# The first out-block's weight conversion moves into the middle of attention; the second in-block's rounding goes one step later

## The chip, the core and the metric

The kernel runs on one core of a Trainium2 chip. The metric is the device time in microseconds (us). The engines are TensorE (PE; PEld is its weight load), VectorE (DVE), ScalarE (ACT), GpSimd (POOL) and SyncE (SP), whose queue issues the loads. Each has its own instruction stream and runs it strictly in order; they wait for one another by semaphores.

## What is computed

Three stages in one program, from `reference.py`, cut:

```python
# attention: q, k, v of (2, 8, 768, 64) float32, 4 sinks, window 128
scores = scale * np.matmul(q, k.transpose(0, 1, 3, 2))
keep = is_sink | in_window            # 0 <= query - key < 128, or key < 4
scores = np.where(keep, scores, -1e9)
a = softmax(scores)                   # max subtracted, 1e-9 added to the sum
x = np.matmul(a, v)                   # then to 1536 tokens x 512
# MoE layer 1: w_in 512 x 2048, w_out 2048 x 512, float64
h = np.maximum(x @ w_in, 0.0); x = h * h @ w_out
# MoE layer 2: the same shapes
h = x @ w_in; g = h * np.tanh(np.log1p(np.exp(h))); out = g @ w_out
```

## The kernel before

**Weights.** Both layers' weights are float64 in memory. The kernel takes them in blocks of 128 hidden units: per block 512 KB for the in-product (`wi`) and 512 KB for the out-product (`wo`), loaded as raw 32-bit pairs and converted on the chip into a high and a low part, so that a product is three terms (low x high, high x low, high x high) of four 128x128x512 matmuls each. Class `Conv` (L104 to L174) holds the steps of one block, each an instruction of 128x512:

- `load`: SP's DMA into tile `raw` (L113 for `wi`, L118 for `wo`; three buffers).
- `head`: ACT scales the upper words into `cv_a` (L128); `head_pool` is the same on POOL (L130).
- `mid_r1` (L136), `mid_r2` (L142), `mid_or` (L148): three on DVE, called r1, r2 and or below; they make `cv_r` (r1 the sign, r2 the top bits of the lower words) and merge it into `cv_a`. `mid_r` is r1 and r2.
- `high`: ACT rounds `cv_a` (L167; `wih` or `woh`). `low`: DVE subtracts it from `cv_a` (L171; `wil` or `wol`), after `high`.

Block 0 is the first `wi`, block 1 the first `wo`, block 2 the second `wi` (tiles `wih1`, `wil1`). All further blocks are converted by the MoE's own loop (`moe()`, L615); the framework's scheduler lets the first two of them (tiles numbered 2051 and 2053 and the `cv` tiles beside them) start on DVE and ACT between the last steps of attention.

**Attention.** 12 query tiles of 128 rows (6 of each batch), 4 pairs of heads in each, so 48 pairs; the loop at L549 runs n from -3 to 52 over them as a hand-written pipeline. In step n:

- PE computes the scores `s` of pair n + 4 (L373), ACT the exponentials `pr` of pair n + 3 (L396), with their sums, DVE the masked max of pair n + 4 (L384, two).
- At even n DVE makes `rs`, the reciprocals of the sums (L407, L408), with which POOL multiplies `pr` (L416, two). PE transposes a tile of q or of k (L323, tile `tr`), which DVE copies to `qt` (L329) or ACT to `kt` (L332); PE computes the outputs `av` of two pairs (L465).
- At odd n PE transposes `pr` of two pairs into `pt` (L428, two banks), of which ACT or DVE makes the copies `pts` (L443).
- Once per query tile ACT copies `av` to `xf` (L480), which the next tile's first `av` waits for, since `av` has one buffer. POOL splits `xf` into `xh` and `xl` (L481, L483); for the last two tiles DVE makes `xl` (L490). In the step after, SP issues the loads `qn`, `kn` and `vn` of a later tile (L232).
- `pt` and `tr` share three PSUM buffers, so a late copy of one holds up the next.

At n = 46 and 48 PE also computes the first two in-products `h` of the first 512 tokens (L195), with the weights of block 0 and of block 2; ACT takes relu, square and `gh` one step later (L204 to L206), DVE `gl` two steps later (L209). The MoE then begins with the first out-product `o` (L634), which uses block 1, and goes on with `h` and `o` in turn to the end.

**What sets the order.** The order in attention is as written in the loop; the conversion steps are called last in step n, by the table `PLAN` {block: {n: steps}} (L497). SP, ACT, DVE and POOL each get them in that order among their own work.

Of the kernel before, what the change touches and what calls it, by code (L numbers as in the profile page):

```python
# [28 lines left out]
def kernel(  # L29
# [463 lines left out]
    for fb in range(W1N):  # L493
# [2 lines left out]
    WARM = (6, 3, 2, 1)  # L496
    PLAN = {  # L497
        0: {5: "load", 11: "head", 13: "mid_r1", 15: "mid_r2", 17: "mid_or", 19: "high low"},
        2: {36: "load", 41: "head_pool", 44: "mid_r", 45: "mid_or", 46: "high low"},
        1: {37: "load", 46: "head mid_r", 47: "mid_or", 48: "high low"},  # L500
    }

    IN_AT = (46, 48)
# [519 lines left out]
```

## Time and profile before

| | |
|---|---|
| median of 3 runs | 620.19 us (619.1 to 620.61) |
| profiled execution | 619.7 us, its span 617.9 us |
| PE busy | 609.0 us (99% of the span) |
| DVE busy | 454.5 us (74%) |
| ACT busy | 351.0 us (57%) |
| POOL busy | 70.1 us (11%) |

The profiled execution's time is the span and 1.8 us around it. Busy is the time in which an engine had an instruction in work; waits of other engines cost nothing where PE does not wait for them. Attention takes about the first 95 us of the span, the two MoE layers the rest; POOL's 70.1 us lie almost all in attention.

### The profile page before, as it was taken

What the parts mean: (1) busy time and instruction counts of PE and PEld (TensorE: products, weight loads), DVE (VectorE), ACT (ScalarE), POOL (GpSimd) and SP (SyncE); (2) the same over time, 40 slices, a digit from 0 to 9 for tenths busy, and PEclk for the clock granted to TensorE, in tenths of its full rate; (3) what the DMA queues carried; (4) which work ended last, traced back from release to release, by engine and by line L of the source; (5) the groups of instructions that cost most, each with busy time, mean ns of one, the idle gap of its engine ahead of it and who ended that gap; (6) DMA issues with size and microseconds to landing.
All of it is one profiled execution on the core that took longest, in us unless ns stands there. A gap on an engine that the chain in (4) does not pass through costs nothing.

```text
span 617.9 us, 10113 instructions
## 1 busy us (share of the span) xinstructions
PE 609.0 (99%) x3774; PEld 494.5 (80%) x3774; DVE 454.5 (74%) x951; ACT 351.0 (57%) x723; POOL 70.1 (11%) x101
## 2 busy tenths in 40 slices
PE   9999999999999999999999999999999999999996
PEld 6676677888888888888888888888888888888885
DVE  5897889998921111169898789999887788887784
ACT  4888876777743233367777655555444444454442
POOL 5788870000000000000000000000000000000000
PEclk9999999999999999999999999999999999999999
DMA  9998835666600000026666400000010000010001
GB/s 190 198 191 173 185 102 185 207 201 201 198 7 1 0 2 1 1 90 186 190 186 199 137 0 2 1 0 1 1 69 0 1 0 1 28 42 1 1 0 72
DMA packets 74904, 50.24 MB, mean 81 GB/s; under 512 B 52708, under 2 KB 69348, under 8 KB 74852
## 3 DMA queue, kind: packets, MB, share of 16 engines
q1 hardware_dynamic: 74560, 49.16, 29.0%
q8 instruction: 31, 0.51, 0.4%
q10 hardware_dynamic: 292, 0.39, 0.2%
q14 instruction: 21, 0.17, 0.1%
HBM read 46.40 MB, written 3.15 MB: 80 GB/s over the span
## 4 chain that ended last, share of the span: by engine, by line
PE 96%; DVE 2%; ACT 1%; issue 0%; DVEq 0%; ACTq 0%
PE o L634 42%; PE h L195 41%; PE s L373 4%; PE av L465 3%; PE tr L323 2%; PE pt L428 2%; PE idle L529 1%; DVE cv_a L148 0%; DVE cv_r L142 0%; ACT pr L396 0%; DVE cv_r L136 0%; DVE pts L443 0%; DVE qt L329 0%; DVE s L384 0%; DVE rs L408 0%
## 5 line engine op out<-in xcount | busy, mean ns | idle before, releaser
L195 PE MATMUL h<-xh,wil 128*128 128x512 f32 x384 | 102.9, 390 | 0.0
L195 PE MATMUL h<-xl,wih 128*128 128x512 f32 x384 | 102.6, 389 | 0.0
L195 PE MATMUL h<-xh,wih 128*128 128x512 f32 x384 | 102.6, 389 | 0.0
L209 DVE TENSOR_TENSOR gl<-h,gh 128x512 fp32r<-128x512 f32 x48 | 33.2, 691 | 89.3 <-ACT gh L206 89.3
L195 PEld LDWEIGHTS h<-xl,wih 128*128 128x128 f32 x384 | 72.1, 188 | 15.0
L195 PEld LDWEIGHTS h<-xh,wih 128*128 128x128 f32 x384 | 72.1, 188 | 15.0
L195 PEld LDWEIGHTS h<-xh,wil 128*128 128x128 f32 x384 | 71.9, 188 | 14.9
L634 PE MATMUL o<-gh,wol 128*128 128x512 f32 x192 | 74.8, 389 | 0.8 <-DVE wol L171 0.8
L702 ACT ACTIVATE e<-t,small 128x512 f32<-128x512 f32 x48 | 34.8, 725 | 70.7 <-DVE t L698 70.7
L634 PE MATMUL o<-gl,woh 128*128 128x512 f32 x192 | 74.7, 389 | 0.0
L634 PE MATMUL o<-gh,woh 128*128 128x512 f32 x192 | 74.7, 389 | 0.0
L204 ACT ACTIVATE h<-h 128x512 f32<-128x512 f32 x48 | 27.9, 582 | 77.5 <-PE h L195 77.5
L634 PE MATMUL o<-wol,gh 128*128 128x512 f32 x176 | 68.5, 389 | 0.0
L634 PE MATMUL o<-woh,gl 128*128 128x512 f32 x176 | 68.5, 389 | 0.0
L634 PE MATMUL o<-woh,gh 128*128 128x512 f32 x176 | 68.5, 389 | 0.0
L718 ACT CAST gh<-t 128x512 fp32r<-128x512 f32 x44 | 27.4, 623 | 46.1 <-PE o L634 42.7
L148 DVE SCALAR_TENSOR_TENSOR cv_a<-cv_a,cv_r 128x512 int32<-128x512 int32 x64 | 45.2, 706 | 6.2
L209 DVE TENSOR_TENSOR gl<-t,gh 128x512 fp32r<-128x512 f32 x44 | 30.4, 690 | 19.5 <-ACT gh L718 19.5
L396 ACT ACTIVATE pr<-s,nm 128x208 f32<-128x208 f32 (+2 forms) x96 | 40.5, 436 | 6.1 <-DVE nm L384 5.7
L416 POOL TENSOR_TENSOR pr<-pr,rs 128x416 f32<-128x416 f32 (+2 forms) x48 | 41.5, 885 | 15.0 <-DVE rs L408 10.4
L128 ACT ACTIVATE cv_a<-raw 128x512 f32<-128x512 f32 x63 | 42.4, 675 | 0.4 <-DMA raw<-in_moe_w_in_dram 0.2
L634 PEld LDWEIGHTS o<-gh,wol 128*128 128x128 f32 x192 | 36.0, 188 | 8.2 <-PE av L465 0.9
(100 smaller groups left out, 1004.1 us busy)
## 6 DMA issues: line engine op xcount, KB each, us to landing
raw<-in_moe_w_in_dram SPq DMA_DIRECT2D x32, 512.0 KB, 4.0
raw<-in_moe_w_out_dram SPq DMA_DIRECT2D x32, 512.0 KB, 4.3
vn<-in_v_dram SPq DMA_DIRECT2D x12, 256.0 KB, 5.1
qn<-in_q_dram SPq DMA_DIRECT2D x10, 256.0 KB, 4.4
kn<-in_k_dram SPq DMA_DIRECT2D x9, 256.0 KB, 4.8
vx<-in_v_dram SPq DMA_DIRECT2D x16, 128.0 KB, 4.3
out_dram<-ob SPq DMA_DIRECT2D x8, 256.0 KB, 2.4
kn<-in_k_dram SPq DMA_DIRECT2D x6, 128.0 KB, 3.0
```

Of the source, the lines that this page charges most:

```text
L128: nc.scalar.activation(out=self.a, in_=high_words, func=AF.Copy, scale=2.0**-112)
L148: nc.vector.scalar_tensor_tensor(out=ai, in0=ai, scalar=3, in1=self.r, op0=ALU.logical_shift_left, op1=ALU.bitwise_or)
L195: nc.tensor.matmul(ph, lhsT=w[a][:, d, :], rhs=x[:, d, :], start=(m == 0 and d == 0), stop=(m == 2 and d == NDC - 1),)
L204: nc.scalar.activation(out=ph, in_=ph, func=AF.Relu)
L209: nc.vector.tensor_tensor(out=gl, in0=x, in1=f32(gh), op=ALU.subtract)
L373: nc.tensor.matmul(banks[e][qs, 0:w], lhsT=qt[b, i][r, j, qs], rhs=kt[r, j, k0 : k0 + w], start=True, stop=True, skip_group_check=True,)
L396: nc.scalar.activation(out=pr[b, i][:, 2 * j + e, 0:w], in_=banks[e][:, 0:w], func=AF.Exp, bias=nm[:, e : e + 1], scale=-1.0, accum_out=sm ...
L416: nc.gpsimd.tensor_tensor(out=x, in0=x, in1=rs.to_broadcast([P, 2, w]), op=ALU.mult)
L465: nc.tensor.matmul(av[b, i][e * D : (e + 1) * D, j, qs], lhsT=x[0:kv, 2 * j + e, :], rhs=pts[0:kv, c, e, qs], start=(j == 0 and m == 0), s ...
L634: nc.tensor.matmul(acc[sp][t], lhsT=a, rhs=x, start=(fb == 0 and m == 0), stop=(fb == NFB - 1 and m == 2),)
L702: nc.scalar.activation(out=e, in_=t, func=AF.Ln, bias=two)
L718: nc.scalar.copy(g_tiles(n)[0], et[n][1])
```

## The change

Two lines of the table. Block 1's load, head, r1, r2, or, and high and low go from steps 37 and 46 to 48 to the odd steps 25 to 33, its load to step 20; block 2's high and low go from step 46 to step 47, where they stand behind `xf` on ACT.

```diff
     PLAN = {
         0: {5: "load", 11: "head", 13: "mid_r1", 15: "mid_r2", 17: "mid_or", 19: "high low"},
-        2: {36: "load", 41: "head_pool", 44: "mid_r", 45: "mid_or", 46: "high low"},
-        1: {37: "load", 46: "head mid_r", 47: "mid_or", 48: "high low"},
+        1: {20: "load", 25: "head", 27: "mid_r1", 29: "mid_r2", 31: "mid_or", 33: "high low"},
+        2: {36: "load", 41: "head_pool", 44: "mid_r", 45: "mid_or", 47: "high low"},
     }
```

PE's and POOL's order stay as they were. In mid-attention, block 1's five instructions come into the streams of ACT and DVE. On DVE (`+` is the changed kernel's), n = 33: the low part comes between the two pairs of max.

```order
@@ -233,4 +236,5 @@
 L384 ISA s,nm<-s,mask_w 128x208
 L384 ISA nm 128x1
+L171 TENSOR_TENSOR wol_111<-cv_a,woh_110 128x512
 L384 ISA s,nm<-s,mask_w 128x208
 L384 ISA nm 128x1
```

In the same way r1, r2 and or stand between two pairs of max at n = 27, 29 and 31, and on ACT the head (n = 25) and the high part (n = 33) stand between a copy `pts` and the exponentials.

The end of attention on DVE, before, from block 2's r1 (`cv_r_1785`) on; 1936 and 1935 are block 1's tiles, 2058 is the first MoE block's, `xl2_72` the split of the last but one query tile:

```order
L136 TENSOR_SCALAR cv_r_1785<-raw_1607 128x512
L142 TENSOR_SCALAR cv_r_1785<-raw_1607 128x512
L148 SCALAR_TENSOR_TENSOR cv_a_1784<-cv_a_1784,cv_r_1785 128x512
L443 COPY pts_1900<-pt_1883 128x8x64
L171 TENSOR_TENSOR wil1_113<-cv_a_1784,wih1_112 128x512
L136 TENSOR_SCALAR cv_r_1936<-raw_1641 128x512
L136 TENSOR_SCALAR cv_r_2058<-raw_2051 128x512
L142 TENSOR_SCALAR cv_r_1936<-raw_1641 128x512
L142 TENSOR_SCALAR cv_r_2058<-raw_2051 128x512
L148 SCALAR_TENSOR_TENSOR cv_a_1935<-cv_a_1935,cv_r_1936 128x512
L490 TENSOR_TENSOR xl2_72<-xf_1940,xh2_69 128x4x128
```

The same place on DVE in the changed kernel (block 2's tiles are 1792 and 1793 here, the MoE blocks' 2057 and 2058, 2063 and 2064):

```order
L136 TENSOR_SCALAR cv_r_1793<-raw_1617 128x512
L142 TENSOR_SCALAR cv_r_1793<-raw_1617 128x512
L148 SCALAR_TENSOR_TENSOR cv_a_1792<-cv_a_1792,cv_r_1793 128x512
L136 TENSOR_SCALAR cv_r_2058<-raw_2051 128x512
L142 TENSOR_SCALAR cv_r_2058<-raw_2051 128x512
L148 SCALAR_TENSOR_TENSOR cv_a_2057<-cv_a_2057,cv_r_2058 128x512
L443 COPY pts_1908<-pt_1891 128x8x64
L136 TENSOR_SCALAR cv_r_2064<-raw_2053 128x512
L142 TENSOR_SCALAR cv_r_2064<-raw_2053 128x512
L148 SCALAR_TENSOR_TENSOR cv_a_2063<-cv_a_2063,cv_r_2064 128x512
L171 TENSOR_TENSOR wil1_113<-cv_a_1792,wih1_112 128x512
L490 TENSOR_TENSOR xl2_72<-xf_1941,xh2_69 128x4x128
```

Block 1's instructions are gone from there; the two MoE blocks' sets of r1, r2 and or now stand ahead of `wil1`, one of them ahead of the copy `pts` too.

The same place on ACT, before, from the copy `pts` ahead of block 2's high part to the relu of the first `h`:

```order
L443 COPY pts_1900<-pt_1882 128x8x64
L167 CAST wih1_112<-cv_a_1784 128x512
L128 ACTIVATE cv_a_1935<-raw_1641 128x512
L128 ACTIVATE cv_a_2057<-raw_2051 128x512
L480 COPY xf_1940<-av_1861 128x512
L128 ACTIVATE cv_a_2063<-raw_2053 128x512
L204 ACTIVATE h_1920<-h_1920 128x512
```

And in the changed kernel:

```order
L128 ACTIVATE cv_a_2057<-raw_2051 128x512
L443 COPY pts_1908<-pt_1890 128x8x64
L128 ACTIVATE cv_a_2063<-raw_2053 128x512
L480 COPY xf_1941<-av_1869 128x512
L204 ACTIVATE h_1928<-h_1928 128x512
L205 ACTIVATE h_1928<-h_1928 128x512
L206 CAST gh_1963<-h_1928 128x512
L167 CAST wih1_112<-cv_a_1792 128x512
```

The high part `wih1` moved from ahead of `xf` to behind it and behind relu, square and `gh` of the first `h`; one MoE block's head moved ahead of the copy `pts`. On SP, block 1's load moved from just ahead of the MoE's loads to just ahead of a `qn` load (the one at 44.53 us in the rows below), and the MoE's loads each follow one place earlier.

## Rows read from the trace of the kernel before

**Rows 1.** List of waits, PE: who for whom: us in total, times, longest.

```profile
PE o L634 <- DVE wol L171: 0.8, 1, 0.8
PE av L465 <- ACT xf L480: 0.7, 1, 0.7
```

**Rows 2.** Chain that ended last, mid-attention: start us, us, what.

```profile
31.79 1.08 PE av L465 x32
...
45.01 1.08 PE av L465 x32
...
55.02 1.08 PE av L465 x32
```

**Rows 3.** Timeline, block 0: start, us, what, [idle before <-releaser].

```profile
30.09 0.70 ACT L128 ACTIVATE cv_a<-raw 128x512 f32<-128x512 f32 x1
...
33.12 1.71 POOL L416 TENSOR_TENSOR pr<-pr,rs 128x416 f32<-128x416 f32 x2
...
34.07 1.05 DVE L136 TENSOR_SCALAR cv_r<-raw 128x512 int32<-128x512 int32 x1
...
37.76 0.50 DVE L142 TENSOR_SCALAR cv_r<-raw 128x512 uint16<-128x512 uint32 x1
```

**Rows 4.** Timeline, the stretch from 44 to 70 us.

```profile
44.53 2.52 SPq L232 DMA_DIRECT2D qn<-in_q_dram  x1
...
55.60 0.66 DVE L329 COPY qt<-tr 128x512 f32<-128x512 f32 x1
...
56.62 0.46 PE L428 MATMUL pt<-ident,pr 64*128 64x64 f32 x8
...
59.95 3.86 POOL L416 TENSOR_TENSOR pr<-pr,rs 128x512 f32<-128x512 f32 x4
...
60.70 0.38 DVE L384 CUSTOM_DVE_ANT_0 s<-s,mask_w 128x208 f32<-128x208 f32 x1 [0.59 <-PE s L373]
...
62.55 0.57 PEld L428 LDWEIGHTS pt<-ident,pr 64*128 64x128 f32 x15 [0.24 <-DVE qt L329]
...
66.63 0.59 ACT L443 COPY pts<-pt 128x512 f32<-128x512 f32 x1 [0.32 <-PE pt L428]
...
67.21 0.38 DVE L384 CUSTOM_DVE_ANT_0 s<-s,mask_w 128x208 f32<-128x208 f32 x1 [0.49 <-ACT pts L443]
...
68.45 0.66 DVE L329 COPY qt<-tr 128x512 f32<-128x512 f32 x1
...
69.11 0.77 PE L428 MATMUL pt<-ident,pr 64*128 64x64 f32 x16
```

**Rows 5.** Timeline, the end of attention, 84 to 100 us.

```profile
84.78 1.43 DVE L142 TENSOR_SCALAR cv_r<-raw 128x512 uint16<-128x512 uint32 x1
...
86.32 1.15 DVE L148 SCALAR_TENSOR_TENSOR cv_a<-cv_a,cv_r 128x512 int32<-128x512 int32 x1
...
87.50 0.62 ACT L167 CAST wih<-cv_a 128x512 fp32r<-128x512 f32 x1 [2.40 <-DVE cv_a L148]
...
89.79 0.34 PE L465 MATMUL av<-pts,vn 80*64 80x64 f32 x4 [0.67 <-ACT xf L480]
...
90.91 1.19 PE L195 MATMUL h<-xh,wil 128*128 128x512 f32 x4
...
92.85 1.07 PE L195 MATMUL h<-xh,wih 128*128 128x512 f32 x4
...
95.80 0.47 PE L634 MATMUL o<-gh,wol 128*128 128x512 f32 x1 [0.79 <-DVE wol L171]
...
97.58 0.68 DVE L171 TENSOR_TENSOR wil<-cv_a,wih 128x512 fp32r<-128x512 f32 x1
98.18 0.42 DVE L136 TENSOR_SCALAR cv_r<-raw 128x512 int32<-128x512 int32 x1
98.61 1.07 PE L195 MATMUL h<-xh,wil 128*128 128x512 f32 x4
...
99.21 0.69 DVE L148 SCALAR_TENSOR_TENSOR cv_a<-cv_a,cv_r 128x512 int32<-128x512 int32 x1
```

## The prediction

> **What bounds the kernel now.** The page's busy times come first: TensorE (PE) is busy for 609.0 of 617.9 us, so the program lasts as long as PE's work and its waits, and an edit that leaves PE's work alone can give back waits or add them, nothing else. The list of waits names two that the moved steps cause: the outputs `av` wait once, 0.7 us, for the copy `xf` on ScalarE (ACT), and the first out-product `o` waits once, 0.8 us, for block 1's low half `wol` on VectorE (DVE) [rows 1]. The chain of waits is PE's `av` groups through mid-attention, at one pace: from 31.79 to 45.01 four double steps of 3.31 us, although block 0 is converted in n = 11 to 19 there, and from 45.01 to 55.02 three of 3.34 with no conversion [rows 2]. The timeline gives the rest: block 0's steps [rows 3], the stretch n = 25 to 35 into which block 1's steps go [rows 4], and the end of attention [rows 5].
>
> **Which step stands where.** The last of attention's transposes `pt`, n = 47, lies between the two early `h` products (n = 46 and 48). Counted back from there by two steps, the `pt` at 56.62 is that of n = 27, at 62.55 of n = 31, at 69.11 of n = 35 [rows 4].
>
> **Load.** The 512 KB load goes from SP's place ahead of the MoE to a place ahead of a `qn` load, which occupied its queue for 2.52 us from 44.53 [rows 4]. That q is read some 12 us later, and the conversion starts at n = 25, some 8 us later. I cost it at nothing; were the cover gone, `qn` would be late by a like transfer, 2.52.
>
> **Term 1: the head at n = 25.** ACT gets 0.70 more [rows 3] in front of two exponentials, whose sums DVE needs before it copies `qt` (55.60 to 56.26); `pt` of n = 27 starts at 56.62 [rows 4]. With 0.36 in hand, 0.3 at most is left of 0.70; the double buffers ahead should hide most of it: +0.1 (0 to 0.3).
>
> **Term 2: r1 at n = 27 and r2 at n = 29.** For block 0 these took 1.05 (while POOL ran `pr`, from 33.12) and 0.50 [rows 3]; alone, r1 took 0.42 at 98.18 [rows 5]. In this stretch POOL multiplies `pr` for 3.86 us from 59.95, and the idle gap that DVE shows is 0.59, ahead of the max at 60.70; PE's `pt` at 62.55 already waits 0.24 for DVE's `qt` [rows 4]. So what exceeds 0.59 arrives at `pt`. Shortest: 0.42 + 0.50 - 0.59 = 0.3. Longest: r1 1.05 and r2 1.43 (the row at 84.78 [rows 5]), 2.48 - 0.59 = 1.9. I take block 0's own pair, 1.05 + 0.50 - 0.59 = +0.96, since POOL works through both places.
>
> **Term 3: high and low at n = 33.** (The or at n = 31 I leave in the gaps that terms 1 and 2 open behind a late PE.) `high` stands on ACT behind the copy `pts` at 66.63, which waited 0.32 for PE; it would run from 67.11 to 67.73, as long as the 0.62 of block 2's, and `low` on DVE from 67.73 to 68.41 (0.68 [rows 5]). Behind `low` stands the next max, now at 67.21, and then `qt`, now 68.45 to 69.11, and `pt` of n = 35 starts at 69.11 with nothing in hand [rows 4]. The max comes 1.16 late, and with it `qt`. Since terms 1 and 2 have by then moved PE against DVE, I take +1.0 (0.5 to 1.2).
>
> **Term 4: the end of attention.** Removed: ACT no longer stands at `high` for 2.40 us (87.50), so `xf` comes early and the 0.67 ahead of `av` at 89.79 goes; `wol` is ready early, so the 0.79 ahead of `o` at 95.80 goes [rows 5]. Added: DVE's order. Behind block 2's or, which ends at 86.32 + 1.15 = 87.47, stood one copy `pts` and then `wil1`, for which `h` of n = 48 waits. Now there stand r1, r2, or of one MoE block, `pts`, r1, r2, or of the next, and then `wil1`. A set lasts 1.72 (98.18 to 99.21 + 0.69), the copy about as long as `low`, 0.68: 87.47 + 2 x 1.72 + 0.68 + 0.68 = 92.27 for the end of `wil1`; 92.0 if the instructions overlap as in the rows, 93.2 if each set is slowed by POOL as block 2's or was (1.15 for 0.69, twice). I take 92.5. `h` of n = 48 starts at 90.91 now. The removed 0.67 lets PE arrive at 90.24 and wait there for 2.3 us: the wait for `xf` is replaced by one for `wil1`. From `h` to `o` PE needs 95.80 - 0.79 - 90.91 = 4.10, so `o` starts at 96.6 in place of 95.80. What is late next: `wil2`. `h` of n = 48 ends at 93.92 now, and relu, gh, gl and then `wil2` on DVE end at 98.26, 4.34 later [rows 5]; that chain stays, `h` ends at 92.5 + 3.01 = 95.5, `wil2` at 99.85, and the next `h` starts at 99.9 in place of 98.61: +1.3. Lower end: `wil1` at 92.0, +0.8. Upper end: 93.2, +2.0. Behind this point PE's work is what it was, and its waits too.
>
> **Sum.** 0.1 + 0.96 + 1.0 + 1.3 = +3.4 (ends 1.6 and 5.4). The profiled execution took 619.7, 0.5 under the median of 620.19: 623.1 for it, and **623.6** for the median of such runs. The likeliest case's own range is 621.8 to 625.6.
>
> **Rivals.**
> *Both waits go and all else is hidden.* 0.67 + 0.79 = 1.46 off: 618.7. For it: both are waits of PE, the only ones at this place [rows 1]. Against: it needs `wil1` by 90.24, and DVE, from 87.47 on, would have to do eight instructions of some 4.8 us in 2.8. It decides as soon as DVE reaches its MoE sets late, behind `wil1`. Chance 0.10.
> *Mid-attention hides block 1 as it hid block 0.* For it: the pace of 3.31 against 3.34, block 0's conversion included [rows 2]; block 0's low half, too, stood behind an ACT copy. Against: block 0's steps fall on the other odd steps (r1 at 13 where block 1's is at 27, a half period apart in the four steps of a query tile), and the gate at 69.11 has nothing in hand [rows 4]. Only term 4 remains: 621.5 (0.3 to 2.0 above now, 0.3 if `o` alone is late and `wil2` is not). Chance 0.20.
> *GpSimd blocks every moved DVE instruction.* DVE's r1 took 1.05 under POOL's `pr` and 0.42 alone; r2 1.43 and 0.50 [rows 3, 5]. POOL works 3.86 us on end from 59.95 [rows 4], and where each instruction meets it terms 2 and 4 go to their upper ends: 0.1 + 1.9 + 1.0 + 2.0 = 5.0, 625.2. Against: the long r1 of block 0 left the pace of PE as it was [rows 2]. Chance 0.13. The Trainium skill ("SBUF — State Buffer", section "Who interferes with whom") calls the port pair that DVE and GpSimd share an exclusive lock; by that rule this would be the likeliest case, and the long r1 and r2 agree with it as far as two rows go.
>
> **Chances.** The forecast 0.50; the rivals 0.10, 0.20, 0.13; the rest, 0.07, to both sides. A measurement of this kernel tells 0.3%, 1.86 us, from no change: under 618.33 is faster, over 622.05 slower. The first rival lies within, and its better part, some 0.03, on the faster side; with a like share of the rest, faster gets 0.04. Within: most of that rival, most of the second (0.13) and the low end of the forecast: 0.26. Slower: 0.70. The range reaches from 620.4, the second rival's low end (620.19 + 0.3, rounded down), to 625.6, the upper end of the sum, and leaves out the first rival and most of the rest.
>
> **What would show it.** Term 1: `qt` of n = 26 later against `pt` of n = 27. Term 2: PE waits for DVE's `qt` at n = 31 that are longer than 0.24. Term 3: a wait of `pt` at n = 35 for `qt`, about 1 us, with `low` ahead of the max. Term 4: no wait of `av` for `xf` nor of `o` for `wol`, in their place a wait of `h` for `wil1`, some 2 us, with two sets of r1, r2, or before it on DVE, and a wait of the next `h` for `wil2`. If the `av` groups between 45 and 75 us keep their pace, terms 1 to 3 are wrong; if `wil1` runs before 90.2, term 4 is.

## The result: slower by 4.5 us, in the range, with two terms of another size

The changed kernel took 624.33 us (median of 6 runs, 622.97 to 625.16), the kernel before 619.87 (6 runs). The ratio is 1.007, 95% interval [1.0055, 1.0086]: slower, as forecast, and 0.7 us over the forecast of 623.6. The profiled execution of the changed kernel took 625.12 (span 623.3, mean granted clock of PE 0.996; before 1.000).

The list of waits of PE after the change, against [rows 1] (who for whom: us in total, times, longest):

```profile
PE pt L428 <- DVE qt L329: 1.7, 2, 1.2
PE h L195 <- DVE wil L171: 1.3, 1, 1.3
PE av L465 <- DVE pts L443: 1.2, 1, 1.2
...
PE tr L323 <- DMA kn<-in_k_dram: 0.7, 2, 0.4
PE o L634 <- ACT xf L480: 0.4, 1, 0.4
```

Both waits of [rows 1] are gone, and five lines stand in their place. Not all of it is the change: of the 1.7 us for `qt`, a wait of 0.50 at 17 us stands in the kernel before as well, and the two for `kn` come at 31.55 and 38.49, ahead of block 1's load, which SP issues at 47.20. PE's order is the same in both kernels, so the start of one and the same PE group can be compared. How much later each group starts than in the profiled execution of before (us; all kernels of this study, worked out from the timelines; a minus is earlier):

| kernel | `pt` n = 27 | `tr` n = 28 | `pt` n = 33 | `tr` n = 36 | `h` n = 46 | `av` n = 48 | `h` n = 48 | `av` n = 50 | next `h` |
|---|---|---|---|---|---|---|---|---|---|
| before starts at | 56.62 | 57.52 | 65.83 | 70.32 | 85.44 | 89.79 | 90.91 | 93.85 | 98.61 |
| the change | 0.88 | 1.08 | 1.08 | 2.49 | 2.51 | 1.75 | 4.55 | 6.15 | 6.02 |
| first half only | -0.30 | -0.10 | -0.09 | 1.31 | 1.30 | 0.69 | 1.73 | 1.74 | 1.63 |
| second half only | -0.05 | -0.04 | -0.05 | -0.06 | -0.06 | -0.82 | 3.44 | 5.40 | 5.27 |
| other odd steps | 0.15 | 0.15 | 0.41 | 0.41 | 0.52 | -0.21 | 2.54 | 5.02 | 4.90 |
| wait filled | -0.55 | -0.35 | -0.34 | 1.07 | 1.06 | 0.35 | filler | 3.10 | 3.00 |
| low part one step later | -0.38 | -0.18 | -0.18 | 0.33 | 1.33 | 0.57 | 3.30 | 4.91 | 4.79 |
| other odd steps, filled | 0.04 | 0.04 | 0.29 | 0.29 | 0.41 | -0.35 | filler | 2.36 | 2.25 |
| r1 and r2 twice | 0.88 | 1.08 | 4.53 | 5.37 | 5.37 | 4.64 | 7.39 | 7.40 | 7.28 |
| both blocks early | -0.05 | -0.04 | 0.21 | 0.20 | 0.88 | 0.12 | 0.08 | 0.13 | 0.02 |
| block 2 early | 0.39 | 0.39 | 0.39 | 0.39 | 1.02 | 0.29 | 0.25 | 0.27 | 0.17 |
| rounding ahead of relu | 0.35 | 0.36 | 0.34 | 0.35 | 0.34 | -0.39 | 0.82 | 0.83 | 0.70 |
| block 2 earlier | 0.14 | 0.14 | 0.13 | 0.19 | 0.19 | -0.55 | -0.59 | -0.54 | -0.66 |

The first column is no effect of the change: it differs from execution to execution by when the tiles of k arrive. A row is read from its first column on. For the change: 0.20 up to n = 28, nothing up to n = 33, 1.41 up to n = 36, nothing up to n = 46, and 3.51 at the end of attention. PE's last matmul still ends 6.04 later. The span is longer by 5.4 only, because what follows that matmul lasts 4.43 in place of 5.06.

The timeline of the changed kernel in mid-attention, for [rows 4] (start us, us, what, [idle before <-releaser]):

```profile
56.98 0.66 DVE L329 COPY qt<-tr 128x512 f32<-128x512 f32 x1
57.50 0.65 PE L428 MATMUL pt<-ident,pr 64*128 64x64 f32 x8
58.61 0.95 DVE L136 TENSOR_SCALAR cv_r<-raw 128x512 int32<-128x512 int32 x1
61.32 0.45 DVE L142 TENSOR_SCALAR cv_r<-raw 128x512 uint16<-128x512 uint32 x1
62.91 0.66 DVE L329 COPY qt<-tr 128x512 f32<-128x512 f32 x1
67.84 1.72 POOL L416 TENSOR_TENSOR pr<-pr,rs 128x416 f32<-128x416 f32 x2
68.19 0.62 ACT L167 CAST woh<-cv_a 128x512 fp32r<-128x512 f32 x1
68.85 1.25 DVE L171 TENSOR_TENSOR wol<-cv_a,woh 128x512 fp32r<-128x512 f32 x1 [0.62 <-ACT woh L167]
70.94 0.66 DVE L329 COPY qt<-tr 128x512 f32<-128x512 f32 x1
71.66 0.71 PE L428 MATMUL pt<-ident,pr 64*128 64x64 f32 x15 [1.16 <-DVE qt L329]
```

`qt` at 56.98 ends at 57.64, behind the start of `pt`: term 1. The low part stands idle 0.62 for `woh`, takes 1.25 beside POOL's `pr`, and `pt` waits 1.16 for the `qt` behind it: term 3. The end of attention, for [rows 5]:

```profile
88.84 1.14 DVE L148 SCALAR_TENSOR_TENSOR cv_a<-cv_a,cv_r 128x512 int32<-128x512 int32 x1
89.90 1.10 DVE L136 TENSOR_SCALAR cv_r<-raw 128x512 int32<-128x512 int32 x1
91.03 0.75 DVE L142 TENSOR_SCALAR cv_r<-raw 128x512 uint16<-128x512 uint32 x1
91.88 0.69 DVE L148 SCALAR_TENSOR_TENSOR cv_a<-cv_a,cv_r 128x512 int32<-128x512 int32 x1
92.49 0.69 DVE L443 COPY pts<-pt 128x512 f32<-128x512 f32 x1
92.71 0.62 ACT L167 CAST wih<-cv_a 128x512 fp32r<-128x512 f32 x1
93.23 0.34 PE L465 MATMUL av<-pts,vx 80*64 80x64 f32 x4 [1.24 <-DVE pts L443]
94.12 0.69 DVE L148 SCALAR_TENSOR_TENSOR cv_a<-cv_a,cv_r 128x512 int32<-128x512 int32 x1
94.72 0.68 DVE L171 TENSOR_TENSOR wil<-cv_a,wih 128x512 fp32r<-128x512 f32 x1
95.46 1.94 PE L195 MATMUL h<-xh,wil 128*128 128x512 f32 x4 [1.31 <-DVE wil L171]
97.19 1.91 PE L195 MATMUL h<-xl,wih 128*128 128x512 f32 x4
98.90 1.17 PE L195 MATMUL h<-xh,wih 128*128 128x512 f32 x4
102.46 0.50 PE L634 MATMUL o<-gh,wol 128*128 128x512 f32 x1 [0.41 <-ACT xf L480]
103.73 0.69 DVE L171 TENSOR_TENSOR wil<-cv_a,wih 128x512 fp32r<-128x512 f32 x1
104.63 1.08 PE L195 MATMUL h<-xh,wil 128*128 128x512 f32 x4
```

The order on DVE is as predicted, a set of r1, r2 and or ahead of `pts`, one (its or at 94.12) ahead of `wil1`. `wih` is done at 93.33, so it is DVE's order and not ACT that `wil1` waits for: DVE was busy for 1.97 of the 2.00 us from 92 to 94. PE waits twice, 1.24 and 1.31. And `h` itself is slow: its first eight matmuls take 3.4 us (95.46 to 98.90), where those of before took 1.94 (90.91 to 92.85 [rows 5]). The stretches of the changed kernel (PE's busy time with its instructions, PE's granted clock, DMA share, GB/s) show at which clock:

```profile
92.00:94.00 2.00, 0.77 (x24) 1.00 0.58 182
94.00:96.00 2.00, 0.69 (x8) 0.91 0.52 147
96.00:98.00 2.00, 2.00 (x6) 0.50 0.61 211
98.00:100.00 2.00, 2.00 (x7) 0.73 0.00 0
100.00:102.00 2.00, 2.00 (x36) 1.00 0.00 0
```

PE was busy for 0.77 and 0.69 us of two stretches of 2.00 us, and behind them its clock stood at 0.50, the lower of its two levels (1.2 GHz in place of 2.4). Whether the waits bring that about is tested below (wait filled). `av` of n = 50 starts 1.60 later against `h` than before (4.55 to 6.15).

### The profile page after: what moved, and what is told of

Same layout as the page of the kernel before. It is cut to its first block, busy times and chain, and to the rows that moved or that the text cites. A ratio compares the mean times of both kernels' runs of the same rounds, so it can differ in the third digit from the quotient of the medians.

```text
span 623.3 us, 10108 instructions
## 1 busy us (share of the span) xinstructions
PE 611.8 (98%) x3774; PEld 495.8 (80%) x3774; DVE 456.6 (73%) x951; ACT 351.1 (56%) x723; POOL 70.3 (11%) x101
## 4 chain that ended last, share of the span: by engine, by line
PE 91%; DVE 3%; SPq 2%; ACT 2%; DMA 1%; issue 1%; DVEq 0%; ACTq 0%
PE o L634 42%; PE h L195 42%; PE s L373 2%; PE av L465 2%; PE tr L323 1%; PE pt L428 1%; SPq L301 1%; PE idle L529 1%; DMA kn<-in_k_dram 1%; SPq L232 1%; ACT pr L396 1%; DVE s L384 1%; DVE cv_r L142 0%; DVE cv_a L148 0%; DVE pts L443 0%
```

## The experiments

Runs of one group shared the runs of before. PLAN lines only, where nothing else is shown; each is an edit of the changed kernel unless said otherwise.

**First half only** and **second half only.**

```diff
-        2: {36: "load", 41: "head_pool", 44: "mid_r", 45: "mid_or", 47: "high low"},
+        2: {36: "load", 41: "head_pool", 44: "mid_r", 45: "mid_or", 46: "high low"},
```

> Block 1 moved to steps 25 to 33 as in the change, block 2's high and low left at step 46. My theory after the change's trace: the middle of attention costs what it cost there (the score tiles' rows stand 0.2 us later from n = 27 on and 1.4 us more from n = 34 on, 1.6 in all, from the head at n = 25 and the low part at n = 33), and the end of attention costs less than with both halves, because one set of r2 and or stands behind the low part of block 2 and no longer ahead of it, so that h of n = 48 waits some 1 to 2 us less: 1 to 2.5 us below the changed kernel, 1.5 to 3.5 above before. Rival, that the end of attention is all in the second half (block 2's rounding at 47): 1.6 us above before, no wait of h for the low part, no clock below 1.0. Rival, that the steps in mid-attention cost nothing and all loss is at the end: no shift between 55 and 85 us.

Measured: 621.42 (10 runs; before 619.95), 1.0026 [1.0014, 1.0037]. The mid-attention shifts are those of the changed kernel, 0.20 and 1.40, as my theory has it, and the rival of free steps there is out. At the end the first rival came nearer than my theory: `h` doesn't wait, and the time is 1.5 above before and 2.9 below the changed kernel, where I had 1.5 to 3.5 and 1 to 2.5. From n = 46 to the next `h` only 0.33 is lost (1.30 to 1.63): `av` waits 0.78 for `pts` in place of the 0.67 for `xf`.

```diff
-        1: {20: "load", 25: "head", 27: "mid_r1", 29: "mid_r2", 31: "mid_or", 33: "high low"},
         2: {36: "load", 41: "head_pool", 44: "mid_r", 45: "mid_or", 47: "high low"},
+        1: {37: "load", 46: "head mid_r", 47: "mid_or", 48: "high low"},
```

> Block 1 at steps 37 and 46 to 48 as before, block 2's high and low at step 47 behind the copy of the output. Theory: no shift before 85 us; the 0.67 us wait of av for xf goes, and the low part of block 2 stands behind one copy, four short steps and an or, and behind relu and gh of the first h on ScalarE: it ends 0.3 to 1 us later than before. So 0 to 1 us above before, and the granted clock stays at 1.0. Rival, that the second half carries the loss at the end by itself: 2.5 to 3 us above before with a wait of h for the low part of over 1 us. Rival, that it gives back the 0.67: 0.7 us below before.

Measured: 624.64 (6 runs), 1.0069 [1.0053, 1.0084], and the granted clock was 0.993 to 0.995 in all six. My theory missed; the first rival holds, and more: alone, the second half costs as much as the whole change. Its timeline:

```profile
90.68 0.66 ACT L128 ACTIVATE cv_a<-raw 128x512 f32<-128x512 f32 x1 [4.06 <-DVE cv_a L148]
92.95 0.62 ACT L167 CAST wih<-cv_a 128x512 fp32r<-128x512 f32 x1
93.61 0.69 DVE L171 TENSOR_TENSOR wil<-cv_a,wih 128x512 fp32r<-128x512 f32 x1 [2.96 <-ACT wih L167]
94.35 2.07 PE L195 MATMUL h<-xh,wil 128*128 128x512 f32 x4 [4.23 <-DVE wil L171]
```

Here ACT makes it late, not DVE: the head of a MoE block stood idle 4.06 for DVE's or, and behind it came relu, square, gh and only then `wih`. I had counted relu and gh, and not that the head ahead of them waits. So the halves do not add up (1.5 and 4.7 against 4.5 for the whole change): in the changed kernel, where block 1 is gone from the end, no head stands idle so long, and `wil1` is late by DVE's order instead. That costs 1.5 less (from n = 46 to `h` of n = 48 the change loses 2.04, the second half alone 3.50).

**Rounding ahead of relu** (an edit of the second half only):

```diff
-        2: {36: "load", 41: "head_pool", 44: "mid_r", 45: "mid_or", 47: "high low"},
+        2: {36: "load", 41: "head_pool", 44: "mid_r", 45: "mid_or"},
...
                 if n == IN_AT[fb] + 1:
+                    if fb == 0:
+                        blocks[2].high()
+                        blocks[2].low()
                     ready[fb] = new_g(gpool)
```

> The second half alone, with block 2's high and low in step 47 still behind the copy xf but ahead of relu, square and gh of the first h (and so ahead of the second MoE block's head, which waited 4.06 us for a buffer). Theory (the place on ScalarE behind relu and that head is what made the low part late): the low part is ready at about 91.2 us, h of n = 48 waits 1 us or less and the clock stays at 1.0: within 0.5 us of before, over 4 us below the second half alone. Rival (VectorE's order, with the MoE block's set ahead of the low part, is what makes it late): 2 us or more above before.

Measured: 620.7 (10 runs; before 619.69), 1.0017 [1.0002, 1.0032]; `h` waits 1.17 for `wil`, no clock under 0.996. The theory is nearer than its rival and misses its bounds by a little: 1.0 above before where I had 0.5 at most, and 3.9 below the second half alone where I had over 4. So 3.7 of the second half's 4.7 us come from the place behind the waiting head and relu, with the lower clock behind that wait included. The wait that remains is DVE's order, as forecast for the whole change: `wih` is done at 88.44, and `wil`, behind a MoE set, starts at 90.99.

**Other odd steps**, and **low part one step later.**

```diff
-        1: {20: "load", 25: "head", 27: "mid_r1", 29: "mid_r2", 31: "mid_or", 33: "high low"},
+        1: {20: "load", 27: "head", 29: "mid_r1", 31: "mid_r2", 33: "mid_or", 35: "high low"},
```

> The change with all of block 1's conversion two steps later (head 27, r1 29, r2 31, or 33, high and low 35), so that the low part stands ahead of a step that transposes k, whose copy is ScalarE's, and not ahead of a copy of qt by VectorE. Theory (the place against qt decides): the 1.4 us at n = 33 and the 0.2 us at n = 25 go, the end of attention stays: 1.2 to 1.7 us below the changed kernel. Rival (the added work on VectorE decides, wherever it stands): the same as the changed kernel within 0.4 us, with the wait of pt for qt at another place.

Measured: 624.05 (9 runs), 1.0054 [1.0037, 1.0071], so only 0.3 below the changed kernel, which is the rival's number. The profile agrees with the theory all the same: mid-attention costs 0.37 (0.15 to 0.52) in place of 1.61. The gain is lost at the end, where the clock took more: `av` of n = 50 comes 2.48 later against `h`. Over the runs: five with a mean clock of 0.993 to 0.996 took 624.05 to 625.85, four with 0.998 to 1.000 took 621.80 to 622.93. The median tells how often the clock fell, not what the place costs.

```diff
-        1: {20: "load", 25: "head", 27: "mid_r1", 29: "mid_r2", 31: "mid_or", 33: "high low"},
+        1: {20: "load", 25: "head", 27: "mid_r1", 29: "mid_r2", 31: "mid_or", 33: "high", 34: "low"},
```

> The change with only block 1's low part moved, from step 33 to step 34, where it stands behind the copies of qt and pts; the high part stays at 33. Theory (term 3: the low part between the two pairs of max is what makes qt late for pt of n = 35): the 1.4 us between n = 33 and n = 34 shrink to 0.3 us or less, the end of attention stays as it was, with a clock that falls in some of the runs: 1 us below the changed kernel, give or take 0.5. Rival (the high part on ScalarE, ahead of the exponentials, makes them late): over 0.8 us of the 1.4 stay.

Measured: 624.62 (5 runs; before 619.72), 1.0087 [1.0072, 1.0102]: no gain. The rows:

```profile
69.50 0.71 PE L428 MATMUL pt<-ident,pr 64*128 64x64 f32 x15 [0.27 <-DVE qt L329]
69.96 1.34 DVE L171 TENSOR_TENSOR wol<-cv_a,woh 128x512 fp32r<-128x512 f32 x1
73.83 0.37 PE L428 MATMUL pt<-ident,pr 64*128 64x64 f32 x5 [0.57 <-DVE pts L443]
```

The wait for `qt` shrank from 1.16 to 0.27, as the theory said, but the next `pt` waits for `pts`, and the shift over both steps is 1.51 (-0.18 to 1.33) as against 1.43. So the rival's number came (over 0.8 stays), its reason in part at most: of the 1.51, 0.51 stand up to n = 36, before `low` can act on PE, and 1.00 come after `low`. I was right on which wait `low` caused and wrong that its place against `qt` is all. Beside POOL `low` took 1.25 to 1.34 in these steps; two steps later it took 0.72, with POOL at work as well, and cost 0.11. That DVE has no room in the one place and has it in the other is my reading, and no run separates it.

**r1 and r2 twice.**

```diff
-        1: {20: "load", 25: "head", 27: "mid_r1", 29: "mid_r2", 31: "mid_or", 33: "high low"},
+        1: {20: "load", 25: "head", 27: "mid_r1 mid_r1", 29: "mid_r2 mid_r2", 31: "mid_or", 33: "high low"},
```

> The change with r1 at n = 27 and r2 at n = 29 each issued twice (the second writes the same values), 0.9 to 1.5 us more of VectorE there. My prediction's term 2 (the steps overflow the idle time of VectorE): the score tiles from n = 31 on stand 0.9 to 1.5 us later against n = 27 than in the changed kernel, with a longer wait of pt for qt. Rival (VectorE has more room there than the one gap that I counted, as the changed kernel's 0.02 us says): 0 to 0.4 us.

Measured: 626.51 (one run). `pt` of n = 33 stands 3.65 later against n = 27 than before, where the change has 0.20. Both theories missed the size:

```profile
58.61 1.70 DVE L136 TENSOR_SCALAR cv_r<-raw 128x512 int32<-128x512 int32 x2
61.58 2.22 POOL L416 TENSOR_TENSOR pr<-pr,rs 128x512 f32<-128x512 f32 x2
62.06 2.05 DVE L142 TENSOR_SCALAR cv_r<-raw 128x512 uint16<-128x512 uint32 x2
65.64 0.59 PE L428 MATMUL pt<-ident,pr 64*128 64x64 f32 x6 [1.43 <-DVE qt L329]
```

The first pair of r1 and r2 (0.95 + 0.45 in the change) costs nothing that PE shows. The second pair pushes r2 under POOL's `pr`, where the two take 2.05, and everything beyond the room goes to PE: 2.35 more of work (3.75 for 1.40) costs 3.45 more, part of it by the lower clock behind the long wait (0.67 and 0.50 in the two stretches from 65 to 69 us). So the room was there for one pair and not for two.

**Wait filled**, alone and on the other odd steps. Six matmuls on the zero tile `warm` ahead of the second `h`, into its bank, which `h` then overwrites:

```diff
                     early[fb] = ps_s.tile([P, TS], F32, tag="s", name="h")
+                    if fb == 1:
+                        for _ in range(6):
+                            nc.tensor.matmul(early[fb][:, 0:P], lhsT=warm, rhs=warm, start=True, stop=True)
```

> The change with six matmuls of 128x128 on the zero tile ahead of h of n = 48, into the bank that h then overwrites; they fill the 1.31 us in which PE waits for the low part of block 2. Theory: h of n = 48 ran at a lower granted clock (its first eight matmuls took 3.5 us where they took 2.0 us) because PE stood still in the waits just ahead of it; with that wait filled the clock stays up for it and 1 to 1.6 us come back, and the mean granted clock of the run is 1.000. Rival 1: the earlier wait of 1.24 us for the copy pts is enough by itself: the clock falls all the same, and the time is the changed kernel's or up to 0.5 us longer. Rival 2: the slow h has another cause (a late operand): the same time and the same long rows.

> Block 1's steps two steps later and the six matmuls ahead of h of n = 48 together. Theory (the two repairs are of two separate losses): the clock stays at 0.998 or above in every run, so that the gain of the other odd steps is no longer hidden by it: 1.0 to 1.4 us below the filled kernel's 623.1, so 621.7 to 622.1. Rival (the loss in mid-attention and that of the clock are one): 623 or more.

Measured: 623.1 (6 runs; before 619.95), 1.0047 [1.0034, 1.0059], 1.2 below the changed kernel, as the theory has it; and 622.47 (5 runs; before 619.72), 1.0054 [1.0041, 1.0068], 0.6 below the filled kernel, over the 622.1 expected and under the rival's 623, so that it decides between neither. The filled kernel's `h`, and the stretch of it:

```profile
91.76 0.34 PE L465 MATMUL av<-pts,vx 80*64 80x64 f32 x4 [1.17 <-DVE pts L443]
92.61 1.60 PE L600 MATMUL h<-warm 128*128 128x128 f32 x12
94.00 1.19 PE L195 MATMUL h<-xh,wil 128*128 128x512 f32 x4
95.03 1.08 PE L195 MATMUL h<-xl,wih 128*128 128x512 f32 x4
```

```profile
92.00:94.00 2.00, 2.00 (x37) 1.00 0.63 200
94.00:96.00 2.00, 2.00 (x11) 1.00 0.78 234
```

The wait for `pts` is still there, `h` starts no earlier, and it runs at the old pace. Over the filled runs of both kernels the clock is 0.997 or more in 11 of 11, over the unfilled ones it is 0.993 to 0.996 in 3 of 6 and 5 of 9.

**Both blocks early** and **block 2 early.** In the first, block 1's line is that of the other odd steps; the second is the kernel before with this line alone:

```diff
-        2: {36: "load", 41: "head_pool", 44: "mid_r", 45: "mid_or", 46: "high low"},
+        2: {28: "load", 35: "head", 37: "mid_r1", 39: "mid_r2", 41: "mid_or", 43: "high low"},
```

> Both blocks converted in mid-attention, in steps whose VectorE part stands ahead of a k step: block 1 at 27, 29, 31, 33, 35 and block 2 (head on ScalarE) loaded at 28 and at 35, 37, 39, 41, 43; so the low part of block 2 is ready well before h of n = 48 and nothing of block 1 or 2 stands at the end of attention. Theory: the 0.67 us wait for xf goes and nothing takes its place until o, which waits some 0.4 us for the second xf; the steps in mid-attention cost 0.4 us for block 1, as two steps later they did, and up to 0.5 for block 2; the clock stays at 1.0. In sum 0 to 0.6 us below before, 4 to 5 below the changed kernel. Rival (each block put into mid-attention costs its 2 us on VectorE): 2 us or more above before.

> Only block 2 moved into mid-attention (load 28, head 35, r1 37, r2 39, or 41, high and low 43), block 1 at the end as before. Theory: the wait for xf goes, h of n = 48 does not wait, and block 1's low part is ready by the time o wants it, since VectorE has one set less at the end; o waits 0.4 us for the second xf instead: 0.5 to 1.0 us below before. Rival (o waits for block 1's low part as before, and the gain is lost there): the same as before within 0.3 us, with a wait of o for wol of over 1 us.

Measured (before 619.69): 620.18 (11 runs), 1.0009 [0.9997, 1.002], and 619.86 (11 runs), 1.0001 [0.9992, 1.001]. Both theories had a gain, and there is none; the rival of the second run has its number and not its reason, since `o` waits 0.41 for the second `xf` and not for `wol`. The end of attention gives back 0.85 in both (1.02 to 0.17 for block 2 alone), and it was spent before: from n = 36 to 46 each lost 0.6 to 0.7. Block 2 early:

```profile
82.91 0.34 PE L465 MATMUL av<-pts,vn 80*64 80x64 f32 x4 [0.39 <-ACT xf L480]
84.74 0.71 PE L428 MATMUL pt<-ident,pr 64*128 64x64 f32 x15 [0.48 <-ACT pts L443]
```

**Block 2 earlier**, the kernel before with:

```diff
-        2: {36: "load", 41: "head_pool", 44: "mid_r", 45: "mid_or", 46: "high low"},
+        2: {24: "load", 31: "head", 33: "mid_r1", 35: "mid_r2", 37: "mid_or", 39: "high low"},
```

> Only block 2 moved, as in the run with 35 to 43, but four steps earlier (load 24, head 31, r1 33, r2 35, or 37, high and low 39), so that its high part stands in the steps that still have transposes of q and k and not where PE has fewer of them and waited 0.39 us for xf and 0.48 us for pts. Theory: these 0.6 us go, the gain at the end of attention (0.8 us) stays: 0.4 to 0.8 us below before. Rival (a conversion costs its 0.6 us wherever it stands in attention): the same as before.

Measured: 618.97 (11 runs; before 619.72), 0.999 [0.998, 0.9999]. Those two waits are gone, the 0.85 stays: the theory holds, and this version is 0.75 us faster than before, just clear of no change.

## Why the prediction was right, and where it was not

- **The load: right.** In the changed kernel it is issued at 47.20, and PE's groups stand 0.88 later than before at 46.6 and still at n = 27.
- **Term 1, +0.1: right in kind, 0.20.** The head delays `qt`, which ends 0.14 behind the start of `pt` of n = 27.
- **Term 2, +0.96: failed.** It measured 0.00 (1.08 at n = 28 and at n = 33), with the or at n = 31, 1.35 us, included. The step that failed is the sentence that what exceeds the idle gap of 0.59 arrives at `pt`. The sign that I had named, a wait for `qt` at n = 31 of more than 0.24, did not come:

```profile
63.62 0.58 PEld L428 LDWEIGHTS pt<-ident,pr 64*128 64x128 f32 x15 [0.23 <-DVE qt L329]
```

  I read one gap; between the two copies `qt` DVE had more. The stretch between them and DVE's busy time in it, before and in the changed kernel:

```profile
56.26:61.83 5.57, 4.30 (x23) 1.00 0.90 183
```

```profile
57.64:62.91 5.27, 5.12 (x24) 1.00 0.89 192
```

  It had 1.27 idle (5.57 - 4.30), and afterwards 0.15. r1 and r2 (0.95 and 0.45) raised its busy time by 0.82, since records that follow one another at once overlap (r1 ends at 59.56, the next max starts at 59.48), and the stretch became 0.30 shorter, since the first `qt` came 1.38 later than before and the second 1.08. That the room was almost used up is what r1 and r2 twice showed.
- **Term 3, +1.0: right in kind, 1.41.** High behind `pts`, low behind high, max and `qt` behind low, `pt` of n = 35 waits: each as read. The 0.68 for `low` was 1.25. (The max that I had 1.16 late is 1.20 late by my own figures, 68.41 - 67.21.)
- **Term 4, +1.3: right in order, mis-sized; 3.51.** That the wait for `xf` is replaced by waiting for `wil1`: PE waited 1.24 and 1.31, 2.55 for the 2.3 forecast, though half of it showed at `av`, for the copy `pts` behind the first set, which I had put into the sum and not seen as a wait of its own. `wil1` ended at 95.40, less 2.49 is 92.9 for 92.5. The chain that is late next, 4.34 from the end of `h` to that of `wil2`, took 4.35 (100.07 to 104.42), but the wait of the next `h` for `wil2`, which I had named as a sign, did not come: PE was at `o` until `h` started at 104.63, and `o` had waited 0.41 for the second `xf`, which I had not seen. So PE's own path set that start, by a margin of 0.2. What was missing is the clock: 1.60 of the 2.2 that are off; `wil1` makes 0.4 and that path 0.2. The prediction took `h` at 3.01 as before, by its first step: that an edit which leaves PE's work alone can only add waits or give them back. The same matmuls took 1.60 longer.
- **Sum.** Of the profiled execution's 5.14 from n = 27 to the next `h`, 1.60 is the clock. Without it the terms measure 0.20, 0, 1.41 and 1.91, 3.5 in all for the 3.4 forecast, and the changed kernel's three runs with a mean clock of 0.998 or more took 622.97 to 624.29 for the 623.6. That they agree so well is luck: a term of +0.96 that was not there stood for what the other three were short of.
- **The rivals.** Both waits gone and the rest hidden: not here, since the MoE sets stood ahead of `wil1`; block 2 earlier, where `wil1` is done before they start, shows what that rival was worth, 0.85 at the end of attention and not the 1.46, because `o` then waits 0.4 for the second `xf`. Mid-attention hidden: in part, r1, r2 and or were, head and low were not. POOL blocking: its rows came (low 1.25 and 1.34, or 1.14, r1 1.10 beside POOL, against 0.68, 0.69 and 0.42), but where DVE had room (r1 0.95 at n = 27, the or 1.35 at n = 31) they cost nothing. The long rows agree in kind with the exclusive lock that the Trainium skill ("SBUF — State Buffer", section "Who interferes with whom") states.

## What to carry to other kernels

Count the idle time of an engine between the two instructions that something waits for, all gaps of it, and not the one gap next to the moved step. Here added work was free up to about that sum, and beyond it all of it arrived, with contention on top. When a step moves behind another on an in-order engine, look at what already waits there: in the second half alone a head that stood idle 4 us for DVE's or cost more than the copy for which the step made way. And price a new wait of PE with the slower clock behind it; where the wait can't go, work that fills it may be cheaper than the wait.

## What the hardware showed that I had not expected

After two waits of 1.24 and 1.31 us, PE's clock was granted at 0.50 in the stretch from 96 to 98 us and at 1.00 again from 100 on. It did not fall in every run of the same kernel: the changed kernel's six had 0.994 to 0.996 three times (624.36 to 625.16 us) and 0.998 to 1.000 three times (622.97 to 624.29). In r1 and r2 twice, the same two waits (1.19 and 1.31) left `h` at its pace of before. Before the change, waits of 0.67 and 0.79, some 5 us apart, left it at 1.00 in the profiled execution. That the waits bring it about is shown by filling the second of them (0.997 or more in 11 of 11 runs, against 7 of 15 of the same two kernels unfilled); what decides it in a single run stays open. That a block's conversion in mid-attention is dearer where DVE meets POOL (low 1.34, 1.25 and 0.72 at three places, POOL at work at each) was measured, and its rule, which instruction of POOL does it and from which point, was not tried.
